# A fused retention and feed-forward kernel on one core: the constants in another order, sixteen pairs by seven products instead of fifteen, and a new list of steps

## The chip, the cores and the metric

The kernel runs on one core of a Trainium2 chip. That core has five engines with a queue of instructions each: TensorE (PE, with its weight loads shown as PEld), VectorE (DVE), ScalarE (ACT), GpSimd (POOL) and SyncE (SP, which here only issues transfers). Sixteen DMA engines move data between HBM and the on-chip SBUF; TensorE writes to PSUM, which has eight banks. The metric is the device time of one execution in microseconds (us), lower is better, given as the median over runs.

## The reference

```python
def _attn_ref(q, k, v):                       # each (8, 8, 576, 64), f32
    scores = (1 / sqrt(64)) * q @ k^T
    gamma = 1.0 - 2.0 ** (-5.0 - arange(H))
    ret = scores * where(rel >= 0, gamma ** rel, 0)      # rel = i - j
    return ret @ v
x = attn_out.transpose(0, 2, 1, 3).reshape(4608, 512)
h = x @ w_in                                  # (512, 2048)
out = gelu_tanh(h) @ w_out                    # (2048, 512) -> (4608, 512)
```

Retention is attention with a decay per head in place of the softmax. Its output is put into 4608 rows of 512 and goes through two dense layers with a GELU between.

## The kernel before, in words

**Retention by chunks.** Each of the 8 batches has 576 positions: four chunks of 128 and a short one of 64. A chunk of all 8 heads is a unit; unit u = 5 * batch + chunk, 40 units in all. The decay is split into a factor on q and one on v, from small tables (`dec`, and `decw` for the wide units), so that a score only has to be masked. What earlier chunks give is carried in a state per head, summed up in f32 and cast to f16 (`sz`). In the first two batches two chunks are taken together as one wide unit (0, 2, 5, 7) with larger packets in their transfers (512 KB per tensor instead of 256); they have a mask of their own, `maskw`, and the others the narrow `mask`. The chunks' result is `xT`, f16, with the 512 columns on the partitions, in a ring of three blocks of 512 tokens.

**First products.** `mm1` makes a block's hidden values from `w_in_sb` and `xT`, GELU on ACT writes `gT`. Blocks 5 to 8 do it by Winograd's form of Strassen's scheme: seven products of half-sized blocks instead of eight, with sums of weight blocks (steps U, `sum_w`, line 961, made once) and of `xT` blocks (s) ahead, and additions behind (l).

**Second products.** `mm2` (line 811) makes 128 tokens by 512 columns with sixteen products from `gT` and `w_out_sb`, in four steps O. The other way takes a pair of such tiles (256 tokens) by seven products (steps W, `product`, line 893): sums of `w_out` blocks (T, once), differences of `gT` blocks (H, `sum_a`, line 875), and seven assemblies (V) of the result. In the kernel before 15 pairs are made so; block 0, and the last half of block 8, are made by O and P. `sum_a` has five forms: 1 to 4 make one difference each, of 128x1024; form 5 makes 1 and 3, which share an operand, in one instruction of 128x2048. The list before uses 1 to 4 alone.

**The list of steps.** The order of all the work behind the constants stands in a string, `ORDER`, one short word per step. Line 1088 reads it and calls the functions, and nothing reorders them: each engine gets its instructions in the order of the list and waits at the head of its queue. The letters that matter here:

- I, J: load a piece of w_in, w_out. POOL issues them, since they convert f32 to f16 on the way. L u,n: load q, k or v (n = 0, 1, 2) of unit u; SP issues these, the stores (S, Q) and the transposing transfers (D), in order.
- q, k, v: scale or cast what was loaded, to f16. t: transpose on PE; y: copy the transpose out of PSUM.
- X, Y, R: a wide unit's key-value sums, its scores (in two parts, which share one PSUM tile with its mask step m), its output. B: the same for a narrow unit. a, o, z: the state; x: the output to xT.
- N and M with F and G: a step of first products (two tiles of 256 tokens; M one tile of 512, or four of 128) and its GELU.
- K n: n products on the identity matrix whose result nobody uses.
- Z: zero one of six `sz` tiles. g, c: constants.

**The pages.** What L loads lies in 21 pages of 256 KB. `page` (line 186) gives out the one that came free the longest time ago, and a load waits until its page's last content has been read. From unit 26 on, and from the first U step on, it gives out only pages 0 to 8:

```python
top = 9 if u >= LATE or sums_on[0] else 3 * NR
```

since the sums of `w_in` (U), of `xT` (s) and some parts of the products lie in pages 9 to 20. In the list before the first U step stands between units 24 and 25.

**The constants.** Ahead of the list stand, in this order: index ramps and the identity in f32 on POOL, the logarithms, the wide tables, the tables of the full chunks, the identity in f16, the masks, the tables of the short chunk. The rows of decay powers are steps: g on VectorE (`gseg`), c on POOL (`gend`).

Of the kernel before, what the change touches and what calls it, by code (L numbers as in the profile page):

```python
# [46 lines left out]
a,15,0 a,15,1 F,2,14,1 j,7,g L,23,1 k,18,g W,1,1,3 N,2,6,1 x,14 V,2,0,0,a z,15,0,v L,18,0 B,16,15
k,17,v W,2,0,6 z,15,1,a V,1,1,6,v F,2,6,1 a,16,0 m,16 x,15 V,1,1,2,a N,3,0,0 V,2,0,1,a v,18,g
N,3,4,0 W,2,1,1 L,17,2 L,24,1 H,2,1,1,v S,1,0 F,3,0,0 N,3,8,0 F,3,4,0 q,18 v,17,v L,19,1 F,3,8,0
N,3,6,0 q,17,g H,2,0,3,v W,2,0,7 q,19,g a,16,1 o,16,1 F,3,6,0 V,2,1,0,v N,3,10,0 D,17 z,16,0,g  # L50
z,16,1,v H,2,1,2,v F,3,10,0 S,1,3 N,3,12,0 B,17,16 W,2,1,6 m,17 V,2,0,3,v x,16 L,21,0 S,1,1
V,2,1,1,v F,3,12,0 N,3,14,0 W,2,0,4 k,19,a H,2,0,4,v N,3,2,0 D,18 V,2,0,5,a F,3,14,0 v,20,g W,2,0,2
L,22,1 L,22,0 a,17,0 W,2,0,5 z,17,0,g H,2,1,4,v a,17,1 D,19 H,2,1,3,v V,2,0,4,v B,18,17 L,20,1
W,2,1,7 j,5,g W,2,0,3 x,17 k,20,g F,3,2,0 z,17,1,v a,18,0 z,18,0,g k,23,a L,22,2 N,3,8,1 F,3,8,1
k,22,a S,1,2 a,18,1 z,18,1,v L,21,1 V,2,0,6,v V,2,1,3,a q,21,g V,2,0,2,a N,3,10,1 N,3,12,1 L,21,2
q,20 L,23,0 F,3,10,1 m,18 B,19,18 W,2,1,4 N,3,2,1 v,19,g V,2,1,5,a F,3,12,1 W,2,1,5 W,3,0,1 D,20
N,3,4,1 x,18 k,21,a F,3,2,1 V,2,1,4,v N,3,14,1 m,19 F,3,4,1 B,20,19 N,3,0,1 H,3,0,1,v F,3,14,1
a,20,0 V,3,0,0,a N,3,6,1 a,20,1 W,2,1,3 m,20 H,3,0,2,v z,20,0,a F,3,0,1 q,22,g v,21,g L,24,2 q,23,g
D,21 H,3,0,3,v L,23,2 v,22,g t,23,q,h F,3,6,1 W,2,1,2 y,23,q,a W,3,0,6 q,24 x,19 V,2,1,2,a V,2,1,6,v
B,21,20 a,21,0 L,26,1 v,24,v j,2,v V,3,0,1,a x,20 z,21,0,a D,22 t,23,k,h a,21,1 z,20,1,a v,23,g  # L60
k,24,g W,3,0,5 S,2,1 L,25,1 L,26,2 m,21 L,26,0 D,24 W,3,0,7 H,3,1,1,v H,3,1,2,v N,4,12,0 B,22,21
x,21 o,21,1 L,25,0 z,21,1,g y,23,k,v a,22,0 z,22,0,a a,22,1 v,26,g W,3,0,2 F,4,12,0 m,22 V,3,0,3,v
M,4,8 L,25,2 V,3,0,4,v B,23,22 m,23 M,4,0 L,27,2 S,2,0 a,23,0 G,4,8 q,25,g q,26 k,25,a M,4,1 x,22
W,3,0,4 S,2,3 G,4,0 D,25 L,28,1 z,22,1,a M,4,9 L,30,0 V,3,0,5,v G,4,1 z,23,0,v H,3,0,4,v G,4,9
N,4,4,0 a,23,1 N,4,6,0 F,4,4,0 B,24,23 F,4,6,0 H,3,1,4,v z,23,1,g M,4,3 M,4,2 W,3,1,1 V,3,0,2,a
U,1,1 W,3,0,3 x,23 m,24 v,25,v H,3,1,3,v L,27,1 G,4,3 M,4,10 B,25,24 k,26,v G,4,2 G,4,10 N,4,12,1
N,4,14,0 V,3,1,0,a k,28,a a,25,0 F,4,12,1 z,25,0,g H,4,0,3,v V,3,0,6,v k,27,g U,2,1 U,4,1 a,25,1
F,4,14,0 L,27,0 W,3,1,5 x,24 N,4,4,1 D,26 q,27 m,25 S,2,2 U,1,0 W,3,1,6 M,4,11 L,28,0 q,30,g B,26,25
F,4,4,1 a,26,0 N,4,14,1 V,3,1,1,a a,26,1 W,3,1,7 U,3,0 m,26 D,27 x,25 W,3,1,2 G,4,11 F,4,14,1
V,3,1,3,a o,26,1 v,27,g L,30,2 V,3,1,4,v L,28,2 L,30,1 W,3,1,4 V,3,1,2,a H,4,0,1,v z,26,0,g U,2,0  # L70
z,25,1,a w B,27,26 a,27,0 N,4,6,1 W,3,1,3 V,3,1,5,v x,26 L,31,0 s,5,1 a,27,1 A,5,0,1 F,4,6,1 W,4,0,1
s,5,2 H,4,0,2,v V,3,1,6,v l,5,0,0,a A,5,0,6 i,2,v s,5,3 l,5,0,1,a A,5,0,2 q,28,g W,4,0,5 V,4,0,0,v
D,28 U,4,0 z,26,1,g z,27,0,a l,5,0,3,v L,29,2 s,5,4 v,28,g m,27 A,5,0,7 A,5,0,5 f,5,0,1 S,3,1 L,29,1
L,29,0 l,5,0,2,a q,29,g W,4,0,6 H,4,1,1,v A,5,0,4 B,28,27 L,31,2 l,5,0,4,v S,3,0 k,29,g f,5,0,0
i,6,v A,5,0,3 H,4,1,2,v V,4,0,1,v A,5,1,1 l,5,1,0,a W,4,0,7 a,28,0 A,5,1,6 W,4,0,2 V,4,0,3,a U,3,1
v,29,g l,5,1,1,a l,5,0,5,v H,4,0,4,v k,30,a a,28,1 f,5,0,2 A,5,1,2 V,4,0,4,v l,5,1,3,v A,5,1,7
W,4,0,4 v,30,g A,5,1,5 l,5,1,2,a x,27 m,28 A,5,1,4 W,4,0,3 f,5,0,3 z,27,1,g f,5,1,0 L,32,1 l,5,1,4,v
V,4,0,2,a q,31 A,5,1,3 l,5,1,5,v V,4,0,5,a j,4,a W,4,1,1 A,5,2,1 A,5,2,2 z,28,0,v D,29 f,5,1,3
V,4,0,6,v l,5,2,0,a V,4,1,0,a H,4,1,3,v L,34,0 B,29,28 f,5,1,1 L,35,1 L,31,1 x,28 A,5,2,6 l,5,2,3,v
W,4,1,6 W,4,1,5 l,5,2,1,a A,5,2,7 D,30 f,5,1,2 H,5,0,3,v f,5,2,1 l,5,2,2,a z,28,1,v k,31,g m,29  # L80
H,4,1,4,v B,30,29 a,30,0 L,32,0 A,5,2,5 V,4,1,1,a k,32,g A,5,2,4 W,4,1,7 v,31,g f,5,2,0 D,31
z,30,0,g m,30 A,5,3,1 x,29 a,30,1 l,5,2,4,v A,5,2,3 l,5,2,5,v l,5,3,0,a B,31,30 j,0,a A,5,3,6
# [48 lines left out]
def kernel(  # L131
# [283 lines left out]
    def decay_rows():  # L415
        power_rows(nc.vector, gseg, SEG)
# [703 lines left out]
```

## Time and profile before

| what | us |
|---|---|
| median of 3 runs | 299.61 |
| lowest and highest | 296.97, 300.61 |
| the profiled execution | 300.45 |
| its span, first to last instruction | 298.7 |
| PE busy | 281.9 |
| VectorE busy | 218.4 |
| ACT busy | 163.4 |
| POOL busy | 109.5 |

| moved | MB |
|---|---|
| from HBM | 36.70 |
| to HBM | 9.44 |
| all packets | 49.51 |

The page shows each engine's busy time, then the span in 40 slices, where a digit is the busy share in tenths. Products on PE overlap in its pipeline, so a product's own length (273 ns for 256 columns) is not its price: eight in a row take 0.87 us. A row of the order of time has the start, the length, engine and line, operation and shape, and in brackets the idle time before it and what ended that. A row of waits has who waited, for whom, how long in all, how often, and the longest. Idle time of an engine that nobody waits for costs nothing.

### The profile page before, as it was taken

The numbers are of one execution on the slowest core, as the hardware profiler recorded it, in microseconds if no ns is written. First come the engines' busy times: TensorE is split into PE (matmuls) and PEld (weight loads), VectorE is DVE, ScalarE is ACT, GpSimd is POOL, SyncE is SP. The second block draws the span as 40 slices with busy tenths as digits, with TensorE's granted clock in tenths as the row PEclk, the third lists the DMA queues.
The fourth block names the chain that finished last, engine by engine and source line by source line (L and its number), as shares of the span: only waits on it lengthen the run. The fifth ranks groups of instructions, "written<-read, shape, count | busy, mean of one in ns | idle before, by whom it ended". The sixth has DMA issues, their size and how long they took to land.

```text
span 298.7 us, 9609 instructions
## 1 busy us (share of the span) xinstructions
PE 281.9 (94%) x4040; PEld 231.1 (77%) x4040; DVE 218.4 (73%) x457; ACT 163.4 (55%) x317; POOL 109.5 (37%) x160
## 2 busy tenths in 40 slices
PE   3885999999999999999999999899999999999995
PEld 1454876767688888888778888788888788788874
DVE  7565781742967578757877998899989899874841
ACT  3251765453426464367755557677747574776420
POOL 5732980042546232382327642641648100000000
PEclk9997999999999999999999999999999999999999
DMA  5999999989999949799996978899998501010113
GB/s 155 265 248 243 229 225 197 208 167 191 225 235 175 192 99 223 169 156 203 241 190 142 187 203 145 191 201 217 174 156 198 147 3 70 4 70 35 72 68 109
DMA packets 135371, 49.51 MB, mean 166 GB/s; under 512 B 117152, under 2 KB 129824, under 8 KB 135328
## 3 DMA queue, kind: packets, MB, share of 16 engines
q1 hardware_dynamic: 130976, 44.71, 70.8%
q0 software_dynamic: 4352, 4.20, 8.6%
q8 instruction: 31, 0.51, 0.7%
q14 instruction: 12, 0.10, 0.1%
HBM read 36.70 MB, written 9.44 MB: 154 GB/s over the span
## 4 chain that ended last, share of the span: by engine, by line
PE 72%; DVE 10%; DMA 7%; SPq 6%; POOL 2%; issue 2%; ACT 1%; DVEq 0%; POOLq 0%; ACTq 0%
PE bank L905 24%; PE bank L791 22%; PE bank L1002 11%; DMA pages<-in_v_dram 5%; PE bank L817 5%; SPq L239 3%; DVE ssum L851 2%; DVE pages L851 2%; PE sk L575 2%; PE x L551 2%; DMA pages<-in_q_dram 1%; PE bank L1032 1%; PE sk L585 1%; SPq L233 1%; PE x L596 1%
## 5 line engine op out<-in xcount | busy, mean ns | idle before, releaser
L791 PE MATMUL bank<-xT,w_in_sb 128*128 128x256 f16 (+2 forms) x624 | 79.0, 278 | 0.2 <-ACT xT L608 0.2
L799 ACT ACTIVATE gT<-bank 128x512 f16<-128x512 f32 x80 | 47.2, 598 | 39.1 <-PE bank L791 38.9
L791 PEld LDWEIGHTS <-w_in_sb 128*128 128x128 f16 x624 | 58.2, 99 | 13.3 <-issue 0.4
L905 PEld LDWEIGHTS <-ssum 128*128 128x128 f16 x480 | 46.3, 98 | 6.7 <-issue 0.6
L905 PE MATMUL bank<-tsum,ssum 128*128 128x256 f16 x360 | 46.1, 273 | 0.2 <-DVE ssum L851 0.2
L905 PEld LDWEIGHTS <-gT 128*128 128x128 f16 x360 | 34.8, 98 | 5.0 <-issue 0.2
L442 POOL TENSOR_TENSOR qk<-pages,dec 128x512 f16<-128x512 f32 (+1 forms) x21 | 22.6, 1081 | 35.0 <-DMA pages<-in_q_dram 19.4
L287 POOL CAST sz<-s 64x256 f16<-64x256 f32 x34 | 17.7, 520 | 40.0 <-DVE s L747 29.4
L905 PE MATMUL bank<-w_out_sb,gT 128*128 128x256 f16 x240 | 31.0, 273 | 0.1
L442 POOL TENSOR_TENSOR v<-pages,dec 128x512 f16<-128x512 f32 (+1 forms) x25 | 26.1, 1050 | 12.6 <-PE x L596 4.5
L1002 PE MATMUL bank<-pages 128*128 128x256 f16 x192 | 28.0, 272 | 0.8 <-DVE pages L851 0.3
L723 DVE TENSOR_TENSOR ret<-sk,mask 128x512 f16<-128x512 f32 (+1 forms) x32 | 19.7, 617 | 11.1 <-PE sk L585 10.2
L1002 PEld LDWEIGHTS <-pages 128*128 128x128 f16 x256 | 24.5, 98 | 4.4 <-issue 1.2
L851 DVE TENSOR_TENSOR ost<-u,bank 128x256 f32<-128x256 f32 x45 | 18.3, 415 | 9.1 <-PE bank L905 5.3
L851 DVE TENSOR_TENSOR ssum<-gT,ssum 128x1024 f16<-128x1024 f16 x30 | 23.3, 776 | 0.2
L851 DVE TENSOR_TENSOR ssum<-gT 128x1024 f16<-128x1024 f16 x30 | 23.3, 777 | 0.0
L851 DVE TENSOR_TENSOR hc<-hc,bank 128x512 f32<-128x512 f32 x29 | 19.8, 682 | 4.7 <-PE bank L1002 2.8
L615 ACT ACTIVATE xT<-x 128x512 f16<-128x512 f32 (+1 forms) x25 | 14.4, 581 | 15.6 <-PE x L596 15.5
L285 ACT COPY hc<-bank 128x512 f32<-128x512 f32 x26 | 15.2, 585 | 13.5 <-PE bank L1002 13.1
L1002 PEld LDWEIGHTS <-w_in_sb 128*128 128x128 f16 x192 | 18.5, 98 | 4.0 <-DVE pages L851 1.3
L817 PE MATMUL bank<-w_out_sb,gT 128*128 128x512 f16 x80 | 19.8, 380 | 0.0
L1002 PE MATMUL bank<-xT,w_in_sb 128*128 128x256 f16 x128 | 19.2, 273 | 0.3 <-DVE hc L851 0.2
(116 smaller groups left out, 453.0 us busy)
## 6 DMA issues: line engine op xcount, KB each, us to landing
out_dram<-ost SPq DMA_DIRECT2D x35, 256.0 KB, 3.0
pages<-in_q_dram SPq DMA_DIRECT2D x32, 256.0 KB, 4.5
pages<-in_k_dram SPq DMA_DIRECT2D x24, 256.0 KB, 5.1
pages<-in_v_dram SPq DMA_DIRECT2D x24, 256.0 KB, 4.5
pages<-in_k_dram SPq DMA_DIRECT2D x4, 512.0 KB, 5.9
pages<-in_v_dram SPq DMA_DIRECT2D x4, 512.0 KB, 10.6
w_in_sb<-in_moe_w_in_dram POOLq DMA_DIRECT2D x8, 256.0 KB, 7.6
w_out_sb<-in_moe_w_out_dram POOLq DMA_DIRECT2D x8, 256.0 KB, 8.6
```

Source lines behind the costliest of these rows:

```text
L239: nc.sync.dma_start(out=r[64 * pp : 64 * pp + 64, 0:4], in_=src[b, 4 * pp : 4 * pp + 4, 128 * c : S, :].rearrange("h s d -> s h d"),)
L285: nc.scalar.copy(out=o, in_=i)
L287: (nc.vector if eng == "v" else nc.gpsimd).tensor_copy(out=o, in_=i)
L442: eng.tensor_tensor(out=out, in0=pages[:, page_of[s["u"], i], 0:n], in1=dec[:, i // 2, s["j"], 0:n].unsqueeze(2).to_broadcast([128, n, D]) ...
L615: nc.scalar.activation(out=xT[:, :, o : o + G * (b - a)].rearrange("c p (h s) -> c p h s", s=G), in_=x[:, a:b].rearrange("c h p s -> c p h ...
L723: nc.vector.tensor_tensor(out=ret[:, :, 0:n], in0=now["two"][:, :, 0, 0:n], in1=mask.unsqueeze(1).unsqueeze(1).to_broadcast([128, 2, n, G] ...
L791: nc.tensor.matmul(hps[:, i, :], w_in_sb[:, ct, 128 * (fc + i) : 128 * (fc + i) + 128], xT[:, ct, TB * t % XR + lo : TB * t % XR + hi], st ...
L799: nc.scalar.activation(out=gTs[t][:, fc : fc + TB // (hi - lo), lo:hi], in_=h.pop((t, fc, lo)), func=AF.Gelu_apprx_tanh, bias=0.0, scale=1.0,)
L817: nc.tensor.matmul(ops[t, tcc], gTs[t][:, ft, 128 * tcc : 128 * tcc + 128], w_out_sb[:, ft, :], start=(ft == 0), stop=(ft == NFC - 1),)
L851: (nc.vector if eng == "v" else nc.gpsimd).tensor_tensor(out=out, in0=a, in1=b, op=op)
L905: nc.tensor.matmul(p["ps", bank][:, HN * col : HN * col + HN], a[:, k], b[:, k], start=(k == 0 and fresh), stop=(k == HK - 1), skip_group_ ...
L1002: nc.tensor.matmul(p["ps", bank][:, n], w[:, c, 128 * n : 128 * n + 128], x[:, c], start=(n == 0 and c == 0 and i in (1, 2, 5)), stop=(c = ...
```

## The change

Three things change.

1. **Constants.** The identity in f16 is made right behind the logarithms, ahead of the wide tables. The wide mask is set to one on POOL instead of VectorE. The tables of the full and the short chunks become one step, b (`tables`), with one exponential on ACT instead of two; the narrow mask goes into step c, beside `gend`; `gseg` is made on POOL (g,g). POOL's index ramps for those tables move behind the wide mask. Steps I that stand at the head of the list would be issued before the constants; the new list begins with another step, so there are none.
2. **Sixteen pairs.** The second half of block 0 is made as a pair by seven products: eight steps O and two result copies go, seven W and seven V come. The T and the first U steps come earlier for it. Twelve of the sixteen pairs take form 5 of the differences (H ...,5) and forms 2 and 4; four pairs take 1 to 4 as before.
3. **The list** is made anew, 1369 steps instead of 1376. The loads of the first units go k4, v0, k0, q0, q2, k2, v2, q4, where they went k4, q2, q0, k0, v0, q4, k2, v2. The pieces of w_in go 6, 7, 2, 3, 1, 0, 4, 5, where they went 1, 0, 2, 3, 4, 5, 6, 7; their first uses go in the same order, and by the step M,0,9 all eight have been used, where the last two were first used by M,0,12. X,2 stands behind N,0,12,0 and N,0,14,0, where it stood behind M,0,0,0 alone. The first U step stands between units 7 and 9, the others up to unit 22. K steps are 38 products, before 36. Some casts and scalings change engine: of 36 q steps POOL has 18 (24 before), of 36 k steps POOL has 13, VectorE 10, ACT 13 (16, 6, 14 before).

```diff
 ORDER = """
-I,1,g g L,4,1 L,2,0 L,0,0 q,2 Z,5,v q,0,g k,4,a L,0,1 L,0,2 k,0,a K,4 K,4 K,4 K,4 K,3 t,0,q,h L,4,0
-I,0,g Z,1,v y,0,q,v Z,3,v K,1,o t,0,k,h t,2,q,h L,2,1 L,2,2 v,0,v y,0,k,a Z,0,g L,5,0 I,2,g K,2,o
-Y,0,0 K,2,o X,0 m,0,0 a,0,1 q,4 a,1,1 K,3,o Y,0,1 Z,2,g m,0,1 k,2,a L,5,1 K,4,o K,4,o t,2,k,h
-z,0,1,v t,4,q,o o,1,1 y,2,q,a R,0 y,2,k,v x,0 Y,2,0 t,4,k,h M,0,0,0 c v,2,v x,1 y,4,k,a m,2,0
-y,4,q,v I,3,g K,1 X,2 I,4,g G,0,0,0 M,0,0,1 L,5,2 z,1,1,g a,2,1 L,4,2 Y,2,1 G,0,0,1 a,3,1 m,2,1
+Z,0,g L,4,1 L,0,2 L,0,1 Z,1,v g,g Z,3,v c k,0,a L,0,0 b I,6,g L,2,0 v,0,v K,4 K,4 K,4 K,4 t,0,k,h
+y,0,k,v q,0,g Z,5,v X,0 I,7,g K,4 K,1 t,0,q,h I,2,g L,2,1 q,2 y,0,q,v a,0,1,g z,0,1,a I,3,g a,1,1
+K,4,o K,3,o Y,0,1 L,2,2 Z,2,g L,4,0 m,0,1 k,2,a K,4 K,2 Y,0,0 m,0,0 o,1,1 t,2,k,h L,5,0 t,2,q,h
+y,2,k,a R,0 L,5,1 I,1,g y,2,q,v x,1 x,0 L,4,2 I,0,g z,1,1,g K,4 Y,2,0 L,5,2 L,7,0 k,4,v v,2,v
+t,4,k,o N,0,12,0 I,4,g N,0,14,0 w y,4,k,a X,2 m,2,0 a,2,1 F,0,12,0 F,0,14,0 L,7,1 a,3,1 Y,2,1 I,5,g
...
     ident_f = const.tile([128, 128], F32, name="ident_f")
     make_identity(nc, ident_f)
+    steps = ORDER.split()
+    while steps[0][0] == "I":
+        load_w_in(int(steps[0].split(",")[1]), "g")
+        steps.pop(0)
...
     for h in range(H):
         nc.vector.memset(lnrow[:, 0, h : h + 1], math.log(gam[h]))
+    ident = const.tile([128, 128], F16, name="ident")
+    nc.vector.tensor_copy(out=ident, in_=ident_f)
...
     tables_wide()
-    nc.vector.tensor_copy(out=idx_f[:, 0], in_=idx_i[:, 0])
...
-    nc.vector.memset(maskw, 1.0)
-    nc.vector.memset(mask, 1.0)
+    nc.gpsimd.memset(maskw, 1.0)
...
+    def tables():
+        nc.vector.tensor_copy(out=idx_f[:, 0], in_=idx_i[:, 0])
...
+        for j in range(3):
+            exponents(j)
+        nc.scalar.activation(out=dec, in_=dec, func=AF.Exp, bias=0.0, scale=1.0)
...
-    def decay_rows():
-        power_rows(nc.vector, gseg, SEG)
-
-    def constants_short():
+    def decay_rows(eng="v"):
+        power_rows(nc.gpsimd if eng == "g" else nc.vector, gseg, SEG)
+
+    def constants_late():
+        nc.gpsimd.memset(mask, 1.0)
...
         power_rows(nc.gpsimd, gend, SEG // 2 + G // 2)
...
-            out=warm, in_=idx_f[:, 0, 0:1], func=AF.Gelu_apprx_tanh, bias=0.0, scale=1.0
+            out=warm, in_=decw[:, 0, 0:1], func=AF.Gelu_apprx_tanh, bias=0.0, scale=1.0
```

More of the change, by code (lines that the diff above doesn't have):

```diff
@@ L413, in power_rows @@
             eng.memset(rows[64 * hl : 64 * hl + 64, hp, :], gam[h] ** n)
[L415 to L418 removed]
+    def decay_rows(eng="v"):
+        power_rows(nc.gpsimd if eng == "g" else nc.vector, gseg, SEG)
+    def constants_late():
+        nc.gpsimd.memset(mask, 1.0)
+        for o in (0, G):
+            nc.gpsimd.affine_select(
+                out=mask[o : o + G], in_=mask[o : o + G], compare_op=ALU.is_ge, fill=0.0, base=0,
+                pattern=[[1, G]], channel_multiplier=-1,
+            )
         power_rows(nc.gpsimd, gend, SEG // 2 + G // 2)
```

264 lines of the change are left out of this document (123 added, 141 removed).

## The prediction

> **What bounds the kernel now.** I read the page first (busy shares, the rows of slices), then the windows, then what PE waits for, and last the order of time of the first 30 us.
>
> ```profile
> PE 281.9 (94%) x4040; PEld 231.1 (77%) x4040; DVE 218.4 (73%) x457; ACT 163.4 (55%) x317; POOL 109.5 (37%) x160
> ...
> DMA  5999999989999949799996978899998501010113
> ```
>
> ```profile
> 21.70:29.00 7.30, 3.10 (x66) 2.68 (x66) 3.31 (x5) 1.94 (x3) 1.20 (x3) 0.77 1.09 255
> 60.00:160.00 100.00, 99.70 (x1510) 81.91 (x1509) 67.50 (x136) 53.42 (x106) 41.20 (x49) 1.00 0.97 191
> 160.00:260.00 100.00, 97.23 (x1462) 85.10 (x1459) 93.19 (x181) 65.69 (x132) 40.00 (x54) 1.00 0.74 144
> 260.00:298.70 38.70, 34.98 (x318) 29.57 (x316) 20.89 (x40) 16.49 (x34) 0.00 (x0) 1.00 0.18 69
> ```
>
> ```profile
> PE x L641 <- DVE wide L458: 4.2, 1, 4.2
> PE bank L1002 <- DVE pages L851: 1.0, 2, 0.6
> PE x L551 <- DVE sz L765: 0.8, 1, 0.8
> ```
>
> In a window the columns are PE, PEld, DVE, ACT, POOL, then granted clock, DMA share and GB/s. From 29 us on PE is the bound: it is idle 0.3 us in 60 to 160, 2.77 us in 160 to 260, and the 3.7 us of the last window are mostly the stores behind the last product. A new order of the steps can win little there. Before 29 us it is otherwise: PE is short of data, the DMA engines are full, and behind a gap of 4.2 us the granted clock is 0.77 over 7.3 us, which is 0.23 x 7.3 = 1.7 us of PE's time. So I price the change in four places: the start, the products' own work, the middle with its pages, and the stretch from 160 us, where VectorE has 93 of 100 us.
>
> **The start.** The order of time, engine by engine (ACT, then VectorE, then PE; start, length, and in brackets the idle time before and what ended it), and a piece of the chain:
>
> ```profile
> 11.39 1.04 ACT L285 CAST wide<-pages 128x1024 f16<-128x1024 f32 x1 [4.88 <-DMA pages<-in_k_dram]
> ...
> 16.68 1.05 ACT L285 CAST wide<-pages 128x1024 f16<-128x1024 f32 x1 [2.52 <-DMA pages<-in_k_dram]
> ...
> 19.88 1.09 ACT L608 ACTIVATE xT<-x 128x512 f16<-128x512 f32 x2 [1.24 <-PE x L699]
> ```
>
> ```profile
> 24.71 1.23 DVE L458 TENSOR_TENSOR wide<-pages,decw 128x1024 f16<-128x1024 f32 x1 [5.03 <-DMA pages<-in_v_dram]
> 25.85 1.22 DVE L666 TENSOR_TENSOR ret_wide<-sk,maskw 128x1024 f16<-128x1024 f32 x1
> ```
>
> ```profile
> 28.95 1.92 PE L791 MATMUL bank<-xT,w_in_sb 128*128 128x256 f16 x16
> ```
>
> ```profile
> 35.50 0.44 PE L641 MATMUL x<-wide,wide 64*64 64x64 f16 x32
> 35.78 0.40 PE L658 MATMUL sk<-qkT 64*64 64x128 f16 x16
> ```
>
> ```profile
> 10.84 13.75 DMA pages<-in_v_dram
> ```
>
> Before, SP's wide loads (512 KB each) go q2, q0, k0, v0, k2, v2, with unit 4's 64 KB pieces between. The second has landed by 9.1 us (q0's row on POOL, further down), the third by 11.4, k2 (fifth) by 16.7 and v2 (sixth) only at 24.6, 13.75 us after its issue. PE has by then done unit 0 and one step of first products, and step X,2 (unit 2's key-value sums) stands ahead of the rest in its queue: that is the 4.2 us gap. After it come the second piece of products and Y,2,1, and the next full product step starts at 28.95. The two rows at 35.50 are the same two steps of unit 5 at full clock.
>
> After the change the wide loads go v0, k0, q0, q2, k2, v2, and unit 4's q follows v2. Unit 0 gains little: k0 takes the second place (9.1), q0 the third (11.4); q0 is still scaled on POOL (1.90) and the copies and masks behind it are those of before, with q2's scaling ahead of y,0,q on VectorE. So I leave the rows of xT where they are, ready at 21.0. Then two whole steps of products (N,0,12,0 and N,0,14,0) stand ahead of X,2, where one half as long stood. At 0.87 each (the chain's row further down) they fill PE to 22.7.
>
> What ends the wait is v2. It keeps its sixth place, so 24.6 is the upper bound. At the spacing of the third from the second, 2.3 us, it would be 9.1 + 4 x 2.3 = 18.3, the lower one. Between lies how much of the DMA engines w_in's loads take, which POOL issues:
>
> ```profile
> 6.46 0.90 POOL L256 DMA_DIRECT2D w_in_sb<-in_moe_w_in_dram  x1
> 9.11 1.90 POOL L458 TENSOR_TENSOR wide<-pages,decw 128x1024 f16<-128x1024 f32 x1 [1.75 <-DMA pages<-in_q_dram]
> 10.96 0.76 POOL L256 DMA_DIRECT2D w_in_sb<-in_moe_w_in_dram  x1
> 11.71 0.54 POOL L408 MEMSET sz<- 128x512 f16 x1
> 12.18 0.72 POOL L256 DMA_DIRECT2D w_in_sb<-in_moe_w_in_dram  x1
> 12.89 0.54 POOL L408 MEMSET sz<- 128x512 f16 x1
> 13.35 1.46 POOL L413 MEMSET gend<- 64x64 f32 x8
> 14.76 1.43 POOL L256 DMA_DIRECT2D w_in_sb<-in_moe_w_in_dram  x2
> ```
>
> ```profile
> 5.90 1.25 DVE L413 MEMSET gseg<- 64x64 f32 x8
> ```
>
> ```profile
> DMA to landing us min/median/max: 6.8/8.1/12.2
> ```
>
> gseg, gend, the narrow mask and one sz are now ahead of the first of these on POOL. 1.25 + 1.46 and under 1 us more move it from 6.46 to about 8.5; the second waits behind q0's scaling, until about 13 instead of 10.96. But six are out by 17 us (before: five by 16.2). v2 therefore has 128 KB less ahead of it and weights that start 2 us later, yet as many beside it. I take 23, near the upper row. From the landing it is 0.1 + 1.23 (scaling) + 1.22 (the mask of Y,2,0, behind it on VectorE) + 0.4 (Y,2,1) = 3.0 us: 26.0 instead of 28.95, at full clock since the gap is now under 2 us. That is **2.95 us won**; with 24.6 it is 1.35, with 20 or less PE itself is the limit (22.7 + 0.44 + 0.40 = 23.6) and it is 5.3.
>
> The Trainium skill, "TensorE: Matmul & The Clock Gate", Part 1, says that the clock falls to half after a window of about 3.4 us without work and rises after one with work. The row of the window 21.7 to 29 agrees. By that rule a gap of 2 us costs no clock, and one of over 3.4 us the 1.7 us once more.
>
> Against it: the eight w_in loads are all needed by M,0,9, some 6 us of PE's work behind the 26.0 (before, the last two were used past 41 us). The last is issued near 21.6, behind unit 1's cast on POOL; with 8.1 to 12.2 us of landing it is there between 29.7 and 33.8, and PE asks at 32.0. Bounds 0 and 1.8 us; I take **0.4 lost**. The warm-up products now wait for an ident that is cast before the tables, so PE starts earlier; that is worth nothing, as k0 is awaited behind them anyway. The short chunks' tables (eight memsets like gseg's 1.25 us and about as much again, some 2.5 us of VectorE) now lie ahead of v0's scaling, while k0 is still on its way; uncovered they would cost their 2.5 us, and they are covered until k0 is cast, 9.1 + 1.05.
>
> **Sixteen pairs instead of fifteen.**
>
> ```profile
> 45.28 0.86 PE bank L817 x4
> ...
> 82.07 0.87 PE bank L905 x8
> ```
>
> Eight plain steps of the first token block's second half (8 x 0.86 = 6.88) go, seven products come (7 x 0.87 = 6.09): **0.79 us won**, all of it on PE. The pair costs VectorE three differences and five of seven assemblies.
>
> ```profile
> L851 DVE TENSOR_TENSOR ssum<-gT 128x1024 f16<-128x1024 f16 x30 | 23.3, 777 | 0.0
> L851 DVE TENSOR_TENSOR ost<-u,bank 128x256 f32<-128x256 f32 x45 | 18.3, 415 | 9.1 <-PE bank L905 5.3 <-ACT xT L615 3.5
> L851 DVE TENSOR_TENSOR pages<-xT 128x512 f16<-128x512 f16 x8 | 4.1, 520 | 0.7 <-PE bank L1002 0.7
> L723 DVE TENSOR_TENSOR ret<-sk,mask 128x512 f16<-128x512 f32 x24 | 16.4, 683 | 2.3 <-PE sk L585 1.4 <-PE x L596 0.9
> ```
>
> That is about 0.78 x 4 + 0.415 x 5 = 5 us, less one copied result, in 50 to 75 us, beside a VectorE that has 67.5 of 100 us: hidden; if not, it delays by what is left over its spare third. In 12 of the 16 pairs two differences are one instruction of 128x2048, which the trace does not show. From 512 (520 ns) to 1024 (777) a step of 512 costs 257, so 2048 gives 777 + 2 x 257 = 1291, against 2 x 777 = 1554: 0.26 saved each, 3.2 us of VectorE in all. Upper bound: the slope of the f32 rows, 683 to 1220 (the mask at 25.85), gives 1220 + 2 x 537 = 2294, 0.74 lost each, 8.9 in all. I take the first, since type and operation are those of its rows.
>
> **The middle and its pages.** The eight sums of w_in (U steps) lie in pages 9 to 20 and the first ran at 152.6 us (rows below); now it stands behind unit 7's loads, ahead of unit 9. From there the page ring has 9 pages instead of 21. Units 9 to 25, which had 21, now load into 9, three units deep. Units 26 on had 9 before, and the stretch where that held, 160 to 260, lost 2.77 us of PE against 0.3 in the one ahead. If all of that were the pages' doing it is 2.5 us lost; the waits name VectorE, so little of it is. I take **1.0 lost**.
>
> **From 160 us.**
>
> ```profile
> L851 DVE TENSOR_TENSOR pages<-w_in_sb x4: 685/828/927, 152.6 to 177.1; 128x1024 f16<-128x1024 f16 x4
> L851 DVE TENSOR_TENSOR pages<-w_in_sb,pages x4: 675/728/883, 159.2 to 172.5; 128x1024 f16<-128x1024 f16 x4
> ```
>
> The U steps (shortest, median, longest in ns, then first and last start) are 4 x 0.83 + 4 x 0.73 = 6.2 us of VectorE, most of it past 159; they move ahead, to between units 7 and 22, where it has room. VectorE's 93.2 becomes about 88. Of PE's 2.77 us of idleness that can win 0 to 2.8; **1.0 won**, since waits for ACT and transfers stay. Six q scalings and four k casts more are VectorE's, most of them POOL's before: ten at the 0.68 of the f32 row, 7 us over the whole run, priced at nothing beside the spare third ahead of 160; uncovered, in the full stretch, it takes the 1.0 back. The last steps and stores are the same kinds in nearly the same order: 0.
>
> **Sum.** 2.95 - 0.4 + 0.79 - 1.0 + 1.0 = 3.3. The profiled execution took 300.45 (span 298.7 and 1.75 around it), so 297.1 on its scale. It stands 0.84 above the median of the runs shown (299.61; they lie between 296.97 and 300.61), which would make it 296.3. I say **296.5**.
>
> **Rivals.** *The weights take the place of the gap* (0.15). v2 lands at 24.6 as before, M,0,9 waits 1.8: 1.35 - 1.8 + 0.79 = 0.3 won, about 299. For it: the sixth place, and six weights out by 17 us. Against: the first two leave later. The Trainium skill, "DMA: Bandwidth & Descriptors", section on queues, rings and completion order, says that each DMA engine takes turns between the queues that have work. By that rule POOL's loads take up to half from SP's whenever both wait, which is the case for 24.6; k2's 16.7 against 9.1 + 3 x 2.3 = 16.0 shows only a little of it, v2's row much.
>
> *Nine pages starve units 9 to 25* (0.12). A load cannot be issued until a page is read, SP is in order, and stores and transposes queue behind it. That each of the 17 units waits 0.7 us makes 12 us: 309. From 0.5 us a unit (8.5) it ends over 2% slower. For it: the row of DMA is at nine tenths through most of the first 30 slices. Against: with nine pages PE lost 2.77 us in 100.
>
> *All of it comes* (0.18): v2 early (5.3), no wait for weights, all 2.8 at the end, no loss to pages: 5.3 + 0.79 + 2.8 = 8.9, 291.5 on the profile's scale; most of it 292 to 293.5.
>
> *The double difference does not save* (0.05): at 2294 ns five of them fall into the full stretch, 3.7 us, and the gain is gone: 300.
>
> **How the numbers follow.** The forecast's own case has 0.50 (294 to 299). Two per cent, about what a measurement of this kernel tells from no change, is 293.6 and 305.6. Faster than that: the third rival, 0.18. Slower: the second, 0.12. The rest, 0.70, lies between. The range leaves out the far end of the third rival and the second: 291.5 to 303.
>
> **What would show it.** Right: no PE wait over 2.5 us past the first product, clock 1.00 from 20 us on, L791 dense from about 26 us; the double difference near 1.3 us; PE idle in 60 to 160 below 1.5 us. Wrong: a wait for DMA ahead of X,2 or M,0,9 of over 3 us with a fallen clock; PE waits behind q, k or v loads between 65 and 160 us; VectorE still above 93 of 100 us past 160.

## The result

The kernel after takes **295.50 us** (median of 17 runs, 294.63 to 298.36), the kernel before 299.38 (17 runs, 296.97 to 300.61). The ratio is 0.989, with an interval of 0.987 to 0.991: 1.1 per cent faster; the medians differ by 3.9 us. The forecast was 296.5. The profiled execution took 295.5, with a span of 293.8, which is 4.9 us less than the 298.7 of before. The profile of before has a mean granted clock of 0.994, and of the 65 runs of before that were taken beside the experiments the 32 at 0.994 or less have a median of 300.0 and the other 33 one of 298.1, while 16 of the 17 runs of after have 0.998 or more.

The page of after, busy time of the engines and the slices of the granted clock and the DMA engines:

```profile
PE 280.0 (95%) x4042; PEld 233.0 (79%) x4042; DVE 225.7 (77%) x446; ACT 166.6 (57%) x325; POOL 95.7 (33%) x157
...
PEclk9999999999999999999999999999999999999999
DMA  6999999949989979999998979997948430110112
```

The windows of after (columns as in the prediction: PE, PEld, DVE, ACT, POOL, clock, DMA share, GB/s), and PE's longest waits from the first product on:

```profile
21.70:29.00 7.30, 5.64 (x123) 4.50 (x122) 3.11 (x4) 3.52 (x7) 1.39 (x3) 1.00 1.20 209
60.00:160.00 100.00, 99.74 (x1605) 87.64 (x1606) 75.11 (x145) 56.04 (x114) 33.90 (x43) 1.00 1.00 197
160.00:260.00 100.00, 96.54 (x1415) 84.67 (x1413) 89.17 (x173) 69.20 (x137) 29.81 (x42) 1.00 0.66 145
260.00:293.80 33.80, 30.46 (x277) 25.42 (x274) 18.49 (x34) 12.00 (x24) 0.00 (x0) 1.00 0.17 63
```

```profile
PE bank L1001 <- DVE pages L850: 1.6, 3, 0.8
PE bank L790 <- ACT xT L607: 0.9, 1, 0.9
PE bank L1001 <- DVE hc L850: 0.8, 2, 0.7
PE bank L790 <- DMA w_in_sb<-in_moe_w_in_dram: 0.7, 1, 0.7
```

In 21.7 to 29 PE is busy for 5.64 us instead of 3.10, at a clock of 1.00 instead of 0.77, and the wait of 4.2 us is gone. In 60 to 160 nothing has changed (0.26 us of idleness, 0.30 before). In 160 to 260 VectorE has 89.17 instead of 93.19, and PE is still idle 3.46 us, more than the 2.77 of before.

What took the place of the wait is told by the chain of after (start, length, what):

```profile
4.84 4.96 DMA pages<-in_q_dram
...
9.97 1.90 POOL wide L457
11.87 1.42 POOL w_in_sb L255 x2
13.28 10.16 DMA w_in_sb<-in_moe_w_in_dram
...
23.49 1.72 PE bank L790 x14
```

Before, the chain ran through v2's landing (10.84 to 24.59). Now it runs through the landing of q0, its scaling on POOL, and a piece of w_in that POOL can issue only behind that scaling and that lands at 23.44. v2 is out of it. Its issue and landing in after (line, length in ns, then the time from issue to landing; issued at 7.42):

```profile
L220 SPq DMA_DIRECT2D pages<-in_v_dram x1: 580/580/580, 7.4 to 7.4; - x1
...
DMA to landing us min/median/max: 8.8/8.8/8.8
```

It lands at 16.2 and is scaled at 19.16, when VectorE comes to it, without a wait; X,2 follows at 21.78:

```profile
19.16 1.22 DVE L457 TENSOR_TENSOR wide<-pages,decw 128x1024 f16<-128x1024 f32 x1
...
19.64 2.21 PE L790 MATMUL bank<-xT,w_in_sb 128*128 128x256 f16 x16
...
21.78 0.45 PE L640 MATMUL x<-wide,wide 64*64 64x64 f16 x32
...
23.49 1.70 PE L790 MATMUL bank<-xT,w_in_sb 128*128 128x256 f16 x14 [0.71 <-DMA w_in_sb<-in_moe_w_in_dram]
```

**A measure of the lead.** To compare kernels whose steps stand in another order, I added up PE's matmuls in order of time, each at its length at full clock (109 ns for 128x256, as in 1.75 us for 16 of them), without the products on the identity that nobody uses, and read off when each profiled execution had done so many us of work. The lead over before, in us:

| work done | before at | after | e1 | e2 | e7 | e8 | e9 | e4 | e12 |
|---|---|---|---|---|---|---|---|---|---|
| 6 us | 28.95 | 5.5 | -5.0 | 1.3 | 2.4 | -0.1 | 1.9 | 1.9 | 6.3 |
| 10 us | 33.22 | 4.4 | -5.0 | 1.3 | 2.2 | -0.1 | 1.9 | 1.9 | 5.4 |
| 25 us | 49.04 | 3.6 | -5.0 | 1.2 | 0.9 | -0.1 | 1.4 | -0.1 | 5.0 |
| 100 us | 127.06 | 3.9 | -4.7 | 0.8 | 1.2 | 0.2 | 1.5 | 0.3 | 5.4 |
| 250 us | 286.22 | 3.5 | -4.5 | 1.1 | 1.8 | 1.0 | 1.7 | 0.5 | 5.8 |

Besides, the whole work of before is 259.1 us by this count and that of after 257.8. So the 4.9 us are 5.5 won at the start, 1.9 of it given back before 50 us, about nothing won or lost behind that, and 1.3 less work. Each column is one execution: before's runs lie over 3.6 us, and its profile is 1.07 us above its median while that of after is at its median. So a lead of 1 us in one profile is no result, and the medians decide.

### The profile page after: what moved, and what is told of

Its sections match the earlier page's. It is cut to its first block, busy times and chain, and to the rows that moved or that the text cites. A ratio compares the mean times of both kernels' runs of the same rounds, so it can differ in the third digit from the quotient of the medians.

```text
span 293.8 us, 9639 instructions
## 1 busy us (share of the span) xinstructions
PE 280.0 (95%) x4042; PEld 233.0 (79%) x4042; DVE 225.7 (77%) x446; ACT 166.6 (57%) x325; POOL 95.7 (33%) x157
## 4 chain that ended last, share of the span: by engine, by line
PE 77%; DVE 11%; DMA 5%; issue 2%; ACT 1%; SPq 1%; POOL 1%; DVEq 0%; POOLq 0%; ACTq 0%
PE bank L904 29%; PE bank L790 21%; PE bank L1001 14%; PE bank L816 4%; DMA w_in_sb<-in_moe_w_in_dram 3%; DVE ssum L850 2%; DVE pages L850 2%; PE sk L574 2%; PE x L550 2%; DMA pages<-in_q_dram 2%; PE sk L584 1%; PE x L595 1%; PE bank L1031 1%; DVE sz L764 1%; DVE hc L850 1%
## 5 line engine op out<-in xcount | busy, mean ns | idle before, releaser
L790 PE MATMUL bank<-xT,w_in_sb 128*128 128x256 f16 (+1 forms) x608 | 79.0, 279 | 1.8 <-ACT xT L607 0.9
L790 PEld LDWEIGHTS <-w_in_sb 128*128 128x128 f16 x608 | 57.5, 98 | 13.2 <-DMA w_in_sb<-in_moe_w_in_dram 2.5
L904 PEld LDWEIGHTS <-ssum 128*128 128x128 f16 x512 | 49.8, 98 | 6.8 <-DVE ssum L850 0.9
L904 PE MATMUL bank<-tsum,ssum 128*128 128x256 f16 x384 | 49.3, 273 | 0.3 <-DVE ssum L850 0.3
L904 PEld LDWEIGHTS <-gT 128*128 128x128 f16 x384 | 37.0, 98 | 4.4
L441 POOL TENSOR_TENSOR v<-pages,dec 128x512 f16<-128x512 f32 (+1 forms) x24 | 24.2, 1010 | 48.5 <-DMA pages<-in_v_dram 26.6
L904 PE MATMUL bank<-w_out_sb,gT 128*128 128x256 f16 x256 | 32.9, 273 | 0.0
L850 DVE TENSOR_TENSOR ssum<-gT 128x2048 f16<-128x2048 f16 (+1 forms) x20 | 21.3, 1063 | 2.7 <-ACT gT L798 2.1
L441 POOL TENSOR_TENSOR qk<-pages,dec 128x512 f16<-128x512 f32 (+1 forms) x16 | 17.1, 1070 | 9.7 <-DMA pages<-in_q_dram 4.8
L746 DVE TENSOR_TENSOR s<-s,sk 128x256 f32<-128x256 f32 x36 | 15.0, 416 | 5.8 <-PE sk L584 4.5
L1019 ACT ACTIVATE gT<-hc 128x512 f16<-128x512 f32 x29 | 17.8, 630 | 2.0 <-DVE hc L850 2.0
## 6 DMA issues: line engine op xcount, KB each, us to landing
w_in_sb<-in_moe_w_in_dram POOLq DMA_DIRECT2D x8, 256.0 KB, 10.2
```

The source lines that it names most:

```text
L441: eng.tensor_tensor(out=out, in0=pages[:, page_of[s["u"], i], 0:n], in1=dec[:, i // 2, s["j"], 0:n].unsqueeze(2).to_broadcast([128, n, D]) ...
L746: nc.vector.tensor_tensor(out=s32, in0=state[0], in1=kv, op=ALU.add)
L790: nc.tensor.matmul(hps[:, i, :], w_in_sb[:, ct, 128 * (fc + i) : 128 * (fc + i) + 128], xT[:, ct, TB * t % XR + lo : TB * t % XR + hi], st ...
L850: (nc.vector if eng == "v" else nc.gpsimd).tensor_tensor(out=out, in0=a, in1=b, op=op)
L904: nc.tensor.matmul(p["ps", bank][:, HN * col : HN * col + HN], a[:, k], b[:, k], start=(k == 0 and fresh), stop=(k == HK - 1), skip_group_ ...
L1019: nc.scalar.activation(out=gTs[t][:, f : f + 2, o : o + 256], in_=p["ps", 0] if i == 0 else p["c", i], func=AF.Gelu_apprx_tanh, bias=0.0, ...
```

## The experiments

### Is it q4's place ahead of k2 and v2? (e1, e3)

SP issues in order, and in before two pieces of q4 stood between v0 and k2. In the chain of before they took 2.55 and 1.30 us to issue instead of 0.6, so k2 and v2 were issued late. e1 is before with this load behind v2; e3 is after with it ahead of k2.

```diff
 e1:
- t,0,q,h L,4,0 I,0,g ... L,2,1 L,2,2 v,0,v
+ t,0,q,h I,0,g ... L,2,1 L,2,2 L,4,0 v,0,v
 e3:
- I,2,g L,2,1 q,2 ... L,2,2 Z,2,g L,4,0 m,0,1
+ I,2,g L,4,0 L,2,1 q,2 ... L,2,2 Z,2,g m,0,1
```

> The kernel before with one load moved: unit 4's q (two pieces of 64 KB) behind v2 instead of ahead of k2. Theory A (v2's place in SP's queue is what made it late: the two small pieces held SP for 2.55 + 1.30 us, and then w_in's loads got in beside v2): v2 lands before 20 us instead of 24.6, the 4.2 us gap of PE ahead of X,2 falls below 1.5 us, the clock stays at 1.00, and the time is 4 to 5.5 us lower, 294 to 295.5. Theory B (the w_in loads beside it hold v2 whatever its place): v2 lands at 23 or later and 0 to 1.5 us are won, 298 to 299.4.

> The changed kernel with unit 4's q back ahead of k2, as before. Theory A: its two pieces hold SP for some 3 us, v2 lands 3 us or more later than the 16.2 us of the changed kernel, 19 to 21, now beside w_in's loads; the scaling of v2, which ran at 19.2, starts at 20 to 21.5 and the time rises by 0 to 2 us: 295.5 to 297.5. Theory B: v2 lands near 17 as the first weights start later in this kernel anyway, and the time stays at 295.5.

e1: 303.21 us, ratio 1.017 (1.010 to 1.025): slower. Its waits and its window:

```profile
PE bank L515 <- DVE qk L442: 5.0, 1, 5.0
```

```profile
21.70:29.00 7.30, 2.42 (x55) 1.80 (x56) 3.40 (x7) 0.37 (x1) 1.45 (x3) 0.59 1.10 263
```

v2 landed at 21.1, 3.5 us sooner, but VectorE scales q4 ahead of everything else that it has to do for units 0 and 2, and q4 now landed at 24.4. A load put back moved the stop to the load itself, and the clock fell to 0.59; neither expectation had this. e3: 295.09 us, ratio 0.990 (0.983 to 0.997), the same as after; v2, issued at 8.82, landed 7.7 us later, at 16.6. Of the 3.42 us between v2's issue in before and in after (10.84 and 7.42) q4's place is thus 1.40; behind after's wide loads its two pieces took 1.29 us to issue instead of 3.85. So q4's place is not what lets v2 land early in after, and in before it cannot be changed alone.

### Is it the gap and its clock? (e2, e7)

e2 fills before's gap with sixteen products on the identity, so that the clock stays up; e7 puts X,2 behind the second piece of products, which then runs in the gap.

```diff
 e2:
- I,3,g K,1 X,2 I,4,g
+ I,3,g K,1 K,16,o X,2 I,4,g
 e7:
- K,1 X,2 I,4,g G,0,0,0 M,0,0,1 L,5,2
+ K,1 I,4,g G,0,0,0 M,0,0,1 X,2 L,5,2
```

> The kernel before with sixteen products on the identity put into PE's gap ahead of X,2, 16 x 0.216 = 3.5 us of the 4.2. If the half clock behind the gap costs what the windows say, 1.7 us come back: 297.7, with the granted clock at 1.00 in 21.7 to 29 us. If the time behind the gap is set by the transfers instead, nothing is won: 299.4 with the clock at 1.00 all the same.

> The kernel before with X,2 moved behind the second piece of the first products (M,0,0,1) in PE's queue; v2's load stays where it was. If the order on PE is what the gain came from: the piece (0.9 us) fills part of the gap, no stretch of over 3.4 us is idle, the clock stays up, and 2.5 us are won, 296.9. If v2's landing is what counts: X,2 still starts at 25.9, and only the piece's 0.9 us and at most the clock's 1.7 are won; by how much of the second tells whether a gap broken in two lets the clock fall: 298.5 if it does, 296.9 if not.

e2: 299.03 us, ratio 1.000 (0.996 to 1.004). e7: 298.96, 1.003 (0.998 to 1.008). The window of e2, and VectorE's scaling of v2 in it:

```profile
21.70:29.00 7.30, 7.30 (x105) 4.73 (x103) 4.52 (x6) 3.02 (x5) 1.84 (x3) 1.00 1.14 249
```

```profile
21.60 1.23 DVE L458 TENSOR_TENSOR wide<-pages,decw 128x1024 f16<-128x1024 f32 x1 [1.03 <-DMA pages<-in_v_dram]
```

The clock did stay at 1.00, and nothing is gained. In this execution v2 landed at 21.5, three us sooner than in the profile of before although the same steps stand ahead of it; where it lands that early, the sixteen products themselves stand in the way. In e7 the new stops are the GELU's copy out of PSUM (1.4 us) and 0.9 us of issue. So neither the clock nor the order of PE's steps is worth much alone; and with the same loads v2 lands up to 3 us apart from one execution to the next (23.7 in e7), which may be why before's times spread as they do.

### Is it the order of the wide loads? (e8, e9)

e8 is before with only k0 and v0 moved to the front of the loads. e9 is before with after's whole order of the wide loads, with the buffers used in the order that this needs, and with the pages that before gave out, written into the kernel.

```diff
 e8:
- L,4,1 L,2,0 L,0,0 q,2 ... k,4,a L,0,1 L,0,2 k,0,a
+ L,4,1 L,0,1 L,0,2 L,2,0 L,0,0 q,2 ... k,4,a k,0,a
 e9:
- L,4,1 L,2,0 L,0,0 q,2 Z,5,v q,0,g k,4,a L,0,1 L,0,2 k,0,a ... L,4,0 ... y,0,q,v ... L,2,1 L,2,2 v,0,v
+ L,4,1 L,0,2 L,0,1 L,0,0 L,2,0 L,2,1 L,2,2 Z,5,v k,0,a v,0,v q,0,g ... L,4,0 ... q,2 y,0,q,v
- a,0,1 q,4 a,1,1 ... z,0,1,v t,4,q,o ... x,0 Y,2,0 t,4,k,h
+ a,0,1 a,1,1 ... z,0,1,v ... x,0 k,4,a q,4 Y,2,0 t,4,q,o t,4,k,h
```

> The kernel before with its loads alone put in another order: k0 and v0 (512 KB in pieces of 512 B) ahead of q2 and q0 (pieces of 2 KB), unit 4's q still ahead of k2. Theory A' (SP is held where too many pieces are under way; with k0 and v0 ahead they drain first, so k2 and v2 are issued by 8.9 us instead of 10.2 and 10.8): v2 lands before 18 us, PE's gap ahead of X,2 falls below 1.5 us, and 2 to 4 us are won, 295.5 to 297.5, less what the later q2 and q0 cost unit 0 (0 to 2 us). Theory B' (w_in's loads, which still leave POOL at 6.5 us, hold v2): v2 lands at 20 or later, nothing is won: 299 to 301.

> The kernel before, with the wide loads in the order of the kernel after (v0, k0, q0, q2, k2, v2, then unit 4's q), the buffers used in the order that this needs (k0, v0 and q0 scaled ahead of q2, unit 4's casts behind x,0), and the pages of the kernel before written out by hand; constants, w_in's loads and all steps from M,0,0,0 on stay as they were. Theory 'both ends at once' (the gain needs v2 early and unit 0's chain not late, and the loads' order with its buffers gives both): v2 has landed by 18.5 us at the latest, no wait ahead of X,2 over 0.5 us, the same work is done 4 to 5 us earlier at 29 us, 3 to 4 of it is left at the end: ratio 0.986 to 0.991, about 296. Theory 'constants and weights' (the order of the tables, and w_in's loads beside the wide ones, hold the start, and the loads' order alone is worth nothing): ratio 0.996 to 1.003, about 299.

e8: 299.29 us, ratio 1.000 (0.997 to 1.002): nothing. Yet v2 lands 8.2 us after its issue at 8.73, at 17.0. The chain of e8:

```profile
6.10 5.08 DMA pages<-in_q_dram
...
11.36 1.90 POOL wide L458
```

q0 is now the last of the first four loads. It lands at 11.18 instead of about 9, POOL scales it 2.25 us later (11.36 for 9.11), and unit 0's chain of transposes, masks and copies comes out 4.5 us later at PE's first products (25.08 for 20.52). Some of these 4.5 us may have another source: PE stood for 3.05 us until that scaling was done, and behind this stop the clock was at half in two windows:

```profile
14.34:17.75 3.41, 2.87 (x32) 1.68 (x30) 2.34 (x3) 2.87 (x3) 3.15 (x13) 0.50 1.15 306
17.75:21.16 3.41, 3.41 (x54) 1.24 (x53) 2.31 (x4) 0.00 (x0) 0.68 (x1) 0.50 1.18 243
```

Three unused products in that stretch took 1.46 us, in before 0.82. How the loss divides between q0 and the clock isn't separated. The stop for v2 is gone and the same time is lost ahead of it: at 6 us of work e8 is level with before.

e9: **296.80 us, ratio 0.988 (0.984 to 0.993)**. The order of the wide loads, with the order of scalings and casts that it needs, and with before's constants, before's places of w_in's loads in the list and before's fifteen pairs, gives what the whole change gives, by its ratio. (In time w_in's loads do move a little: the second leaves POOL at 11.86 us instead of 10.96, since q0, whose scaling stands ahead of it, lands later.) Its v2 and its chain:

```profile
L223 SPq DMA_DIRECT2D pages<-in_v_dram x1: 592/592/592, 7.4 to 7.4; - x1
...
DMA to landing us min/median/max: 8.7/8.7/8.7
```

```profile
6.16 5.00 DMA pages<-in_q_dram
...
11.67 1.32 DVE wide L460
12.99 1.15 DVE qkT L289
```

v2 lands at 16.1, and X,2 runs without a stop. Unit 0's chain is late by 2.7 us in the profile (its first products at 23.22 for 20.52; the rows show q2's scaling on VectorE ahead of the copy that the chain needs, and the clock is at half from 13.98 to 17.40), less than in e8. The profiled execution of e9 took 298.71, the longest of its seven runs (the shortest 296.11), so the lead of 1.7 in the table probably understates it.

### Do w_in's loads hold k2 and v2? (e4)

After with four of w_in's eight loads (256 KB each) issued from 6 us on, ahead of step c (`gend` and the narrow mask) and of q0's scaling.

```diff
- g,g Z,3,v c k,0,a L,0,0 b I,6,g L,2,0 ... X,0 I,7,g K,4 K,1 t,0,q,h I,2,g L,2,1 ... z,0,1,a I,3,g
+ g,g Z,3,v I,6,g I,7,g I,2,g I,3,g c k,0,a L,0,0 b L,2,0 ... X,0 K,4 K,1 t,0,q,h L,2,1 ... z,0,1,a
```

> The changed kernel with four of the w_in loads (6, 7, 2, 3) moved ahead of the narrow mask and gend on POOL, so that they leave at 6.1 to 8.9 us instead of 8.25 to 14.0. Theory A': v2, issued at 7.4 us, still lands by 18.5, the weights land 2 to 3 us earlier, PE's wait for them (0.9 us at 22.5) goes: 0.5 to 1.5 us won, 294 to 295. Theory B': v2 and k2 land 4 us later or more (20 or past it), X,2 waits for it, and 1 to 4 us are lost: 296.5 to 299.5.

299.19 us, ratio 0.998 (0.993 to 1.002): nearly all of the gain is gone. One row of its chain:

```profile
7.43 16.51 DMA pages<-in_v_dram
```

SP issued k2 and v2 at 6.79 and 7.43, as in after (6.78 and 7.42); k2 landed at 18.3 instead of 13.0, and v2 at 23.9 instead of 16.2. So it isn't the issue alone: what POOL has under way beside them takes its share. The Trainium skill, "DMA: Bandwidth & Descriptors", section on queues, rings and completion order, says that each DMA engine takes turns between the queues that have work; e4 agrees. POOL's later issues also pushed q0's scaling back (11.35 for 9.97), so that unit 0's chain is 3 us late as well: PE's first products start at 22.61 instead of 19.64, and its wait at X,2 is only 0.79 us. How the loss divides between v2, k2 and q0's scaling isn't separated.

### What is the sixteenth pair worth? (e5, e10)

Both are after with the second half of block 0 by eight plain steps. In e5 the steps simply took the products' places:

```diff
- W,0,1,1 ... W,0,1,5 ... W,0,1,6 ... W,0,1,7 ... W,0,1,4 ... W,0,1,3 ... W,0,1,2
+ O,0,8 ... O,0,9 ... O,0,10 ... O,0,11 e,0,2,v ... O,0,12 ... O,0,13 ... O,0,14 O,0,15 e,0,3,a
- H,0,1,* V,0,1,* (all)
 e10, against e5:
- O,0,11 e,0,2,v ... S,0,3 ... S,0,2
+ O,0,11 ... O,0,12 ... e,0,2,v ... S,0,2 ... S,0,3
```

> The changed kernel with the second half of block 0 made by eight plain steps, as before, in the places of the seven products; the seven assemblies and three differences go, two result copies come. If the products' own work is what the pair is worth: 0.79 us slower, 296.3, with the order of everything else kept. If VectorE's 4 us for the pair delayed something: no difference or faster, 294.5 to 295.5.

> The kernel after, with block 0's second half by eight plain steps in the places of the seven products, its results copied by VectorE some steps behind the last product that they need, and the stores of its two blocks changed over so that the ring of output tiles goes round in the order in which they are taken. If the sixteenth pair is worth what its products say, PE's work grows by 8 x 0.86 - 7 x 0.87 = 0.8 us and the time is that of the kernel after plus 0.8 (ratio about 0.992). If the pair's differences and results on VectorE cost what its products save, the time is that of the kernel after (0.989); if VectorE's load in 50 to 75 us mattered, it is faster than that.

e5: 307.34 us, ratio 1.027 (1.022 to 1.031), a measure of its own faults and not of the pair. VectorE's copy of a result stood ahead of a state's cast in its queue, and PE stopped 1.9 us; then an output tile was still waiting for its store, and PE stopped 4.4 us (`ost`). What the first of them did to the clock is the one thing in it worth keeping; the window and PE's order of time in e5:

```profile
70.00:80.00 10.00, 9.22 (x136) 5.75 (x137) 6.89 (x11) 4.16 (x10) 2.69 (x3) 0.83 0.65 122
```

```profile
69.97 0.29 PE L549 MATMUL x<-qkT,sz 128*128 128x64 f16 x4 [1.87 <-DVE sz L763]
...
70.69 1.89 PE L789 MATMUL bank<-xT,w_in_sb 128*128 128x256 f16 x8
72.37 1.78 PE L815 MATMUL bank<-w_out_sb,gT 128*128 128x512 f16 x4
73.99 1.04 PE L789 MATMUL bank<-xT,w_in_sb 128*128 128x256 f16 x8
```

Behind a stop of 1.87 us, with PE full on both sides, eight products of 128x256 took 1.89 us instead of 1.04, and the clock of that window is 0.83.

e10: 297.19 us, ratio 0.991 (0.988 to 0.994), beside 0.989 for after. PE's work is 258.6 us by the count above, 0.8 more than after's 257.8. That count follows from the list of steps. Whether the time follows it isn't settled: the ratios say 0.6 us, with intervals that overlap (0.988 to 0.994, and 0.987 to 0.991), and the medians, each beside other runs of before, 1.7 us (297.19 and 295.50), while e10's products wait 1.9 us for w_in and those of after 0.7. That the pair's differences and assemblies on VectorE cost as much as its products save doesn't show.

### Does the double difference, or VectorE's load past 160 us, matter? (e6)

After with each double difference made as two of 128x1024.

```diff
- H,0,1,5,v
+ H,0,1,3,v H,0,1,1,v
 ... (in all twelve pairs that had one)
```

> The changed kernel with the twelve double differences split into two of 128x1024 each. VectorE gets 12 x 0.25 = 3 us more, five of them in the full stretch from 160 us. If VectorE bounds that stretch: 1.2 us slower, 296.7, and PE's idle time there 1 us more than 3.5. If it does not, 295.5 within 0.5.

295.98 us, ratio 0.989 (0.985 to 0.993): the same as after. The groups of VectorE in after, and the late window of e6:

```profile
L850 DVE TENSOR_TENSOR ssum<-gT,ssum 128x1024 f16<-128x1024 f16 x32 | 24.0, 754 | 0.1
...
L850 DVE TENSOR_TENSOR ssum<-gT 128x2048 f16<-128x2048 f16 x12 | 15.4, 1282 | 2.3 <-ACT gT L798 2.1
```

```profile
160.00:260.00 100.00, 96.62 (x1413) 84.41 (x1411) 88.84 (x177) 68.70 (x137) 30.40 (x42) 1.00 0.67 145
```

The double difference takes 1282 ns, so it saves about what was forecast, and it doesn't reach the time. In this window all differences together take 20.40 us of VectorE in e6 and 19.14 in after, and PE is idle 3.38 and 3.46 us.

### Can the start of after be mended? (e11, e12)

The two stops that are left at its start are a piece of w_in issued behind q0's scaling, and the copy x that waits for a step of products. e11 moves I,7 ahead of q,0, R,2 and the copies ahead of the step N,0,4,0, and Y,0,0 ahead of six products on the identity; e12 leaves the last of these out.

```diff
- y,0,k,v q,0,g Z,5,v X,0 I,7,g K,4
+ y,0,k,v I,7,g q,0,g Z,5,v X,0 K,4
- N,0,6,0 N,0,4,0 F,0,4,0 q,4,g F,0,6,0 R,2 x,3 t,4,q,o x,2
+ N,0,6,0 R,2 F,0,6,0 N,0,4,0 x,3 x,2 q,4,g F,0,4,0 t,4,q,o
 e11 only:
- k,2,a K,4 K,2 Y,0,0 m,0,0
+ k,2,a Y,0,0 K,4 K,2 m,0,0
```

> The kernel after with three moves that aim at the waits that its start still has: w_in's load I,7 ahead of q0's scaling on POOL (into 0.8 us of idleness there), Y,0,0 ahead of six warm-up products, and R,2 with the copies behind it ahead of the step N,0,4,0. If PE's order and the weights are what its start waits for, the waits of 0.7 us for w_in and 0.9 us for xT go and the first mask comes 0.5 us sooner: 1 to 2 us, about 294 (ratio 0.982 to 0.986). If v2 and k2 then land later by the weight that goes ahead of them and this decides, nothing is won (0.989) or 1 us is lost.

> The kernel after with two of the three moves of e11_start (w_in's load I,7 ahead of q0's scaling on POOL; R,2 with the copies behind it ahead of the step N,0,4,0); the warm-up products stay between Y,0,1 and Y,0,0, since in e11_start Y,0,0 waited 1.3 us there for VectorE's mask and the transposes of k2 came 1.5 us later. If e11_start's median (ratio 0.981) came from these two moves, this one has it too, and half a microsecond more: 293.5 to 294.5, ratio 0.979 to 0.983. If the profile of e11_start is right that its lead is gone by 46 us, the time is that of the kernel after: ratio 0.987 to 0.990.

e11: 294.33 us, ratio 0.981 (0.977 to 0.986). e12, beside other runs of before (median 298.06): 294.71, ratio 0.990 (0.985 to 0.995). In the profile e11 has lost its lead over after by 46 us and its span is after's (294.1), while e12 keeps 2.2 us to the end (span 291.6). The one wait of e12's products on w_in:

```profile
PE bank L790 <- DMA w_in_sb<-in_moe_w_in_dram: 0.3, 1, 0.3
```

Both medians are about 1 us below that of after and both lie below before's, but the two ratios, which differ only by the place of six idle products, lie 0.9 per cent apart, with intervals that hardly overlap. By its ratio e11 is ahead of after (0.981 and 0.989) and e12 is not (0.990). So whether either beats after isn't settled.

## Why the prediction was right

The total was right, 296.5 against 295.5, and the place was right: the start. Several terms behind it were off, and they made up for one another.

- **The start, 2.95 forecast, 5.5 measured: mis-sized.** The step that failed is "I take 23, near the upper row". v2 landed at 16.2, below even the lower row of 18.3, whose spacing of 2.3 us between wide loads was too long (k0, k2 and v2 of after land at 8.5, 13.0 and 16.2). What came is the prediction's other case, "with 20 or less PE itself is the limit", which it had at 5.3. The reasoning said "yet as many beside it" of w_in's loads. But v2 was issued at 7.42 instead of 10.84, of which q4's place is 1.40 (e3) and the order of the wide loads the rest, and only one load of w_in landed ahead of it (at 15.6), where four had in before (14.4, 17.7, 20.2 and 23.3). e4 puts that crowd back, and v2 lands at 23.9. "Unit 0 gains little" was nearly right: the first products start at 19.64 instead of 20.52. e8 shows that this needed watching: with v2 as early and unit 0 late, nothing is left. Both ends of the 5.5 are single profiles, and that of before holds its half clock (25.53 to 28.94 us).
- **w_in's loads, 0.4 lost forecast, 1.9 given back.** The mechanism of the first rival came, at another place: the stop is not at M,0,9 but at the steps ahead of it, and the load in question is not the last but the fourth, issued by POOL behind q0's scaling. Its wait of 0.7 us ends at 23.49 and so lies inside the 5.5, which would be 6.2 without it. Of the 1.9 given back behind it the waits name 0.9 for xT, which the chain of after puts behind that load (products, GELU, copy), and 0.5 for a sum of the state; what the rest is isn't shown. So the start nets 3.6 where 2.55 was said.
- **The pair, 0.79: right by PE's count.** 0.8 us of PE's work by e10; its time doesn't settle it.
- **The pages, 1.0 lost: 0.** PE is idle 0.26 us in 60 to 160 with nine pages from unit 9 on, and no q, k or v load shows among its waits.
- **The late stretch, 1.0 won: 0.** VectorE's 93.19 became 89.17, and PE's idleness 3.46 instead of 2.77. PE's waits there name single results (`pages`, `hc`), each a step of a chain; e6 adds 1.26 us of differences there and changes neither PE's idleness nor the time. That they wait for the length of a chain and not for VectorE's load is argued from these rows; no run took the U steps back alone.
- **Not in the sum:** about 0.5 us less PE work beside the pair. The list of after has two PE transposes (t) fewer, and one transposing transfer (D) more in their place.

So 2.55 + 0.79 - 1.0 + 1.0 = 3.3 was said, and 3.6 + 0.8 + 0 + 0 + 0.5 = 4.9 is what the profiles show; the medians, with their own spread, show 3.9. The two terms that were nothing cancelled in the sum, which is luck.

What was to be seen held: no wait over 2.5 us behind the first product (the longest is 0.9), clock 1.00 from 20 us on, the double difference at 1282 ns (1291 said), PE idle 0.26 us in 60 to 160, VectorE below 93. Full steps on L790 do not run dense from 26 us but from 23.5, with one stop.

## What to carry to other kernels

At a start where data is short, ask of each load when it can be issued, what is under way beside it from other queues, and which chain waits for it; two chains that meet have to come early together, since either one alone (e8, e1) moves the stop instead of removing it. Count a term for a busy engine only where the waits show that its load, and not the length of a chain on it, ends them.

## What the runs showed of the hardware that was not expected

- A stop of 1.87 us between full stretches was followed by half the clock for 3.41 us in e5 (70.48 to 73.89), some 1.7 us lost. The prediction took a gap under 2 us for free. The Trainium skill, "TensorE: Matmul & The Clock Gate", Part 1, speaks of an idle window of about 3.4 us; here a shorter one was enough, and the measurement decides. The length of the stop alone doesn't tell: one of 2.12 us in after, ending at 9.58, and one of 2.59 in e12, ending at 9.93, cost no clock. In the 3.41 us ahead of the fall PE was busy for 1.54 us in e5, 1.28 in e9, 1.03 in e8 and 0 in before; in 5.70 to 9.11 of after, which holds most of that stop, it was 1.75.
- The half clock lasted 3.4 us in before (25.53 to 28.94) and in e9, 6.8 in e8, and 10.2 in e1 (23.02 to 33.26): one, two and three times the same length.
- The issue of a 64 KB load on SP took 0.6 us at first and 2.55 or 1.30 us in before behind two wide loads of k and v; in after the same load took 3.07 us behind k2 and v2. It looks as if what a queue has under way holds the next issue, so the place of a small load matters to those behind it.
- The same v2, issued at 10.84 and 10.87, landed at 24.6 in before and at 21.5 in e2, with the same steps ahead of it. In e2 q0 landed 0.7 us later, so that w_in's second and third loads left POOL at 11.65 and 12.88 instead of 10.96 and 12.18. That this is the reason isn't shown: in e7 they left at 10.44 and 11.66, and v2 landed at 23.7.
